# Two changes to a three-stage kernel: the first 256 tokens run through the network with float32 products, and the first solve stays on VectorE

## The chip, the cores and the metric

One NeuronCore of a Trainium2 chip runs the whole program; the other cores idle. The metric is the device time of one execution in microseconds (us). Engines are written as in the profile: PE is TensorE, PEld its loads of stationary operands, DVE is VectorE, ACT is ScalarE, POOL is GpSimd, SP is the queue that issues nearly all transfers.

## The reference, cut to what matters

Three stages follow each other; the first is a recurrence over 768 positions for 32 heads, the other two are networks over the 3072 tokens that it leaves.

```python
for t in range(S):                                   # 4 batches, 8 heads, S=768, D=48
    y[:, :, t] = einsum('bhd,bhde->bhe', q[:, :, t], state)
    v_old = einsum('bhde,bhd->bhe', state, k_n[:, :, t])
    state = state + beta_t * outer(k_n[:, :, t], v[:, :, t] - v_old)
x = y as (3072, 384)
g = s * relu(x @ w_in)**2 + b                        # w_in 384 x 2048, float64 in memory
x = g @ w_out                                        # w_out 2048 x 384, float64 in memory
e = argmax over 8 experts of the cosine of x and expert_emb
out = gate * relu(x @ w1[e]) @ w2[e]                 # 384 x 1024 x 384
```

## The kernel before, in words

**Stage one, the recurrence.** Positions are cut into chunks of C=32. Four chunks of all heads form a group `gi`; there are six, of 512 tokens each. For a group the kernel transposes keys and queries (`tr_kn` or `tr_k`, `tr_q`), forms their products (`gram`, for the first group `gram_first`), moves them into one 32x32 problem per lane of VectorE (`lanes_in`) and inverts a unit triangular matrix there. `solve(gi, j)` is one of 31 steps over the whole 32x32 matrix: a product into `tmp` and a subtraction from `T`, both on VectorE. For groups 0 and 1 the kernel takes another way: `solve_d` does 15 such steps on the two 16x16 diagonal blocks at once, and the block below them is made by TensorE: `off_in` transposes twice, `off_1` and `off_2` are 32 products per chunk each, with an eviction between them. The result is `tt`. Then four `dstep`s per group go through the chunks, each a chain: `ks` (TensorE, state times keys), X (VectorE), `tx` (TensorE, with `tt`), bdu (VectorE), `ku` (TensorE), the state `sst` (VectorE); `mu` makes the output tokens, which ACT copies to `x_t`.

**Stage two, the first network,** is `moe1`, over twelve groups `kk` of 256 tokens. `x_split` transposes the tokens and splits them into a high and a low part in fp32r (`xh`, `xl`). `mm1(kk, j)`, j from 0 to 7, does 256 of the 2048 hidden features: 6 pairs (f, m), and for each three fp32r matmuls (high by high, high weight by low x, low weight by high x). ACT takes relu, POOL squares and applies s and b, ACT and VectorE split the result into `gh` and `gl`. `mm2(kk, j)` is 18 fp32r matmuls into `acc`. Both are generators with six steps of three matmuls; a group has 96 steps. `mm2(kk, j)` is emitted after `mm1` of two pairs later.

**Weights.** They come as float64, in 16 pieces of 128 x 768 values (even pieces of `w_in`, odd of `w_out`; `W_ORDER` is the order of use). A piece is turned into float32 by two ACT scalings (`w_scale`), two VectorE bit operations and one POOL addition into a separate buffer `wa`; then `w_parts` has ACT cast the high part and POOL subtract for the low part. `convert` does this in two `w_step`s per piece, `convert_piece` both. `poll` lets group 1 of the tokens be split only when all pieces are converted.

**Order.** On PE, DVE, ACT and POOL the order of emission is the order of execution. `attention` holds a list of items with due times for each group, and yields between them; the main loop then calls `run_moe(n)`, which emits n steps of `moe1`, and every fifth step one `w_step`. While group 0 is in its four chunks there are no tokens yet; the items there are the rest of `off_2`, `k_rows` and eight conversions. Items with times from 99 on prepare group 1: transposes, `gram`, the router, `lanes_in(1)`, 15 `solve_d`, `off_in`, `off_1` and `off_2`; after each the main loop emits 2, 12, 3, 10 or 1 steps of `moe1`, 97 in all, which is the whole of token group 0 and the start of group 1. From `gi=1` on the number of steps for each quarter of a hop is set by what is left (24*KF//2*gi - 36 steps by the end of a group). `warm` are matmuls without a use for their result. Transfers are issued by SP in an order that the framework chooses near the order of emission.

Of the kernel before, what the change touches and what calls it, by code (L numbers as in the profile page):

```python
# [19 lines left out]
def tile_kernel(ctx, tc, q, k, v, beta, w_in, w_out, s_in, b_in, emb, tau, w1, w2, out):  # L20
# [60 lines left out]
    def xh_ring(shape, dt, name):  # L81
        t = mp.tile([128, 2, KD, TT], dt, tag="xhl", name=name, bufs=2)
        if len(shape) == 4:
            return t
        return t.rearrange("p a k t -> p (a k t)")[:, 0:shape[1] * shape[2]].rearrange("p (a b) -> p a b", b=shape[2])
# [111 lines left out]
    def gc_tile(gi):  # L197
        if gi == 1:
            gc_t[gi] = att.tile([128, B, 2, HG, C], F32, tag="kqt", name="gc", bufs=KQB)
        elif gi:  # L200
            gc_t[gi] = stg.tile([128, B, 2, HG, C], F32, tag="gc", name="gc")
        else:
            gc_t[gi] = xh_ring([128, 32, C], F32, "gc").rearrange("p (h g n) t -> p h g n t", h=B, g=2)
# [40 lines left out]
    def lanes_in(gi):  # L244
        if gi < 2:
            Af = stg.tile([128, C + 1, C], F32, tag="A", name="A")
            Tf = T0[0] if gi == 0 else stg.tile([128, C + 1, C], F32, tag="gc", name="T")
# [4 lines left out]
        if gi > 1:  # L252
            Tf = T = stg.tile([128, C, C], F32, tag="gc", name="T")
# [63 lines left out]
    def off_in(gi):  # L317
        A, T = ln.pop(gi)
        tt_t[gi] = att.tile([128, 2 * HG * B, C], F32, tag="tt", name="tt", bufs=2)
# [5 lines left out]
    def off_1(gi, n0, n1):  # L325
# [8 lines left out]
        if gi:  # L334
            zz = stg.tile([128, 2 * B, n1 - n0, C2], F32, tag="tmp", name="zz")
        else:
            if n0 == 0:
                of["z"] = mp.tile([128, 2, TT], F32, tag="gl", name="zz", bufs=2).rearrange(
                    "p a t -> p (a t)").rearrange("p (n e i) -> p n e i", n=HG, i=C2)
            zz = of["z"][:, n0].unsqueeze(2)  # L340
# [133 lines left out]
    def attention(more, first):  # L474
        for gi in range(NG):
# [5 lines left out]
            if gi == 0:  # L481
                add(0, off_2, 0, 1, 2)
                add(0, first)
                add(0.1, k_rows, 0, 1)
                add(1, off_2, 0, 2, 3)
                add(1.1, convert_piece)
                add(2, off_2, 0, 3, 4)
                add(2.1, k_rows, 0, 2)
                add(4.1, k_rows, 0, 3)
                for i in range(3, 3 * HG - 2):  # L490
                    if i % 3 != 2:
                        add(i, convert_piece)
                add(10, convert_piece)
            if gi + 1 < NG:
# [747 lines left out]
```

## Time and profile before

| | before |
|---|---|
| three timed runs | 1018.87, 1020.95, 1022.46 us; median 1020.95 us |
| the profiled execution | 1018.81 us, of it 1017.1 us between first and last instruction |
| mean granted clock of TensorE | 0.917 of full |
| busy, share of the span | PE 86%, PEld 79%, DVE 48%, ACT 32%, POOL 30% |
| chain that ended last | the last three instructions on the output, 0.1% each |

The chain of waits reaches back only to the last output tile, so it does not say what bounds the middle; the windows and the waits of TensorE do. A busy share of PE counts pipelined matmuls as one block; mean ns of one matmul includes the latency that overlaps its neighbours, and the price of one in a row is busy time over count.

### The profile page before, as it was taken

To read this page: it belongs to the slowest core of one execution; us is meant where nothing else is said; L and a number is where in the kernel's file an instruction comes from. 1 tells how busy PE (TensorE), PEld (TensorE's weight loads), DVE (VectorE), ACT (ScalarE), POOL (GpSimd) and SP (SyncE) were. 2 spreads that over 40 slices of the span, in tenths; PEclk is the share of its full clock that TensorE was granted. 3 is DMA by queue.
4 is the path that set the end of the run, shared out by engine and by line. 5 is a ranking of instruction groups with operands and counts; after the bars stand their busy time and mean duration, and the time that the engine had idled before them with its cause. 6 is when DMAs were issued, how large, how long until landed. Compare 5 with 4: busy or idle time off the path is not lost. (4 is left out here: it accounts for less than half of the span.)

```text
span 1017.1 us, 29943 instructions
## 1 busy us (share of the span) xinstructions
PE 875.7 (86%) x13213; PEld 801.1 (79%) x13213; DVE 484.9 (48%) x984; ACT 324.7 (32%) x689; POOL 301.8 (30%) x294
## 2 busy tenths in 40 slices
PE   6468646496699799979998999999998889889997
PEld 4355646495599799979898889999997679779896
DVE  3638499425953596259725873224414333331111
ACT  2127634123135133423342333334422222222221
POOL 4116568312122333233323333334540110110100
PEclk7558788679699899999999999999999999999999
DMA  8791133001122012101200000003202901114000
GB/s 149 219 291 30 25 50 60 3 19 34 23 45 49 3 36 46 41 11 34 48 18 3 18 2 17 3 17 94 79 17 49 42 24 51 51 36 175 16 32 24
DMA packets 119826, 50.35 MB, mean 50 GB/s; under 512 B 94167, under 2 KB 116368, under 8 KB 119696
## 3 DMA queue, kind: packets, MB, share of 16 engines
q1 hardware_dynamic: 112784, 47.23, 20.2%
q10 hardware_dynamic: 6336, 1.18, 0.8%
q8 instruction: 104, 1.70, 0.7%
q14 instruction: 26, 0.21, 0.1%
q0 software_dynamic: 576, 0.02, 0.0%
HBM read 38.84 MB, written 9.74 MB: 48 GB/s over the span
## 5 line engine op out<-in xcount | busy, mean ns | idle before, releaser
L678 PE MATMUL h<-xhl,wp 128*128 128x256 f32 x1728 | 250.9, 295 | 43.4 <-ACT r L686 29.8
L678 PEld LDWEIGHTS h<-xhl,wp 128*128 128x128 f32 x1728 | 224.0, 199 | 50.4 <-ACT r L686 32.6
L687 POOL TENSOR_TENSOR r<-r 128x512 f32<-128x512 f32 x96 | 106.3, 1108 | 350.8 <-ACT r L686 350.8
L710 PE MATMUL acc<-gh,wp 128*128 128x256 f32 x1152 | 161.4, 286 | 1.7 <-POOL wp L595 1.7
L710 PEld LDWEIGHTS acc<-gh,wp 128*128 128x128 f32 x1152 | 146.1, 193 | 3.4 <-POOL wp L595 2.0
L690 DVE TENSOR_TENSOR gl<-r,gh 128x512 fp32r<-128x512 f32 x96 | 74.2, 773 | 130.6 <-ACT gh L689 130.4
L689 ACT CAST gh<-r 128x512 fp32r<-128x512 f32 x96 | 59.8, 623 | 161.0 <-POOL r L688 158.3
L952 DVE SCALAR_TENSOR_TENSOR hl<-h,hh 128x512 fp32r<-128x512 f32 x46 | 31.7, 691 | 139.2 <-ACT hh L951 139.2
L686 ACT ACTIVATE r<-h 128x512 f32<-128x512 f32 x96 | 57.4, 598 | 97.3 <-PE h L678 69.5
L710 PE MATMUL acc<-gl,wp 128*128 128x256 f32 x576 | 84.6, 283 | 0.2 <-DVE gl L690 0.2
L688 POOL TENSOR_SCALAR r<-r,s_sb,b_sb 128x512 f32<-128x512 f32 x96 | 81.1, 845 | 10.0
L710 PEld LDWEIGHTS acc<-gl,wp 128*128 128x128 f32 x576 | 75.2, 193 | 0.5 <-DVE gl L690 0.4
L437 ACT COPY x<-ch 32x384 f32<-32x384 f32 x96 | 45.2, 471 | 69.7 <-PE ch L423 68.7
L1021 POOL TENSOR_TENSOR x2l<-xr,x2h 128x512 fp32r<-128x512 f32 x15 | 18.7, 1279 | 164.0 <-ACT x2h L1020 164.0
L1032 PE MATMUL o<-w2h,hh 128*128 128x384 f32 x184 | 62.3, 339 | 0.0
L1032 PE MATMUL o<-w2l,hh 128*128 128x384 f32 x184 | 61.9, 336 | 0.0
L1032 PE MATMUL o<-w2h,hl 128*128 128x384 f32 x184 | 61.8, 336 | 0.0
L292 DVE TENSOR_TENSOR T<-T,tmp 128x31 f32<-128x31 f32 (+15 forms) x124 | 54.6, 440 | 4.3
L289 DVE TENSOR_TENSOR tmp<-A,T 128x31 f32<-128x31 f32 (+15 forms) x124 | 55.1, 445 | 2.9
L949 PE MATMUL h<-x2l,w1h 128*128 128x512 f32 x120 | 49.6, 414 | 6.5 <-POOL x2l L1021 6.5
L951 ACT ACTIVATE hh<-h 128x512 fp32r<-128x512 f32 x46 | 27.4, 598 | 83.4 <-PE h L949 83.4
L949 PE MATMUL h<-x2h,w1h 128*128 128x512 f32 x120 | 48.4, 403 | 6.1 <-ACT x2h L1020 4.9
(212 smaller groups left out, 1260.3 us busy)
## 6 DMA issues: line engine op xcount, KB each, us to landing
wr<-in_moe_w_in SPq DMA_DIRECT2D x16, 384.0 KB
wr<-in_moe_w_out SPq DMA_DIRECT2D x8, 768.0 KB
v<-in_v SPq DMA_DIRECT2D x192, 24.0 KB
x2d<-x2s SPq DMA_DIRECT2D x24, 192.0 KB
out<-o SPq DMA_DIRECT2D x24, 192.0 KB
qpad<-in_q SPq DMA_DIRECT2D x40, 96.0 KB
kpad<-in_k SPq DMA_DIRECT2D x160, 24.0 KB
xr<-x2d SPq DMA_DIRECT2D x5, 768.0 KB
```

Of the source, the lines that this page charges most:

```text
L289: nc.vector.tensor_tensor(out=tmp, in0=A[:, j + 1:, j:j + 1].to_broadcast([128, m, j + 1]), in1=T[:, j:j + 1, 0:j + 1].to_broadcast([128, ...
L292: nc.vector.tensor_tensor(out=T[:, j + 1:, 0:j + 1], in0=T[:, j + 1:, 0:j + 1], in1=tmp, op=ALU.subtract)
L437: nc.scalar.copy(out=x_t[gi][pb:pb + C, :, r * 96:(r + 1) * 96].rearrange("p h (g e) -> p h g e", g=2), in_=y[32 * rr:32 * rr + 32, :, :, ...
L678: nc.tensor.matmul(out=h[:, f, :], lhsT=wi_(w, 2 * j + f, m), rhs=x[:, m, :], start=(m == 0 and i == 0), stop=(m == KD - 1 and i == 2))
L686: nc.scalar.activation(out=r, in_=h, func=AF.Relu)
L687: nc.gpsimd.tensor_tensor(out=t, in0=r, in1=r, op=ALU.mult)
L688: nc.gpsimd.tensor_scalar(out=t, in0=t, scalar1=s_sb, scalar2=b_sb, op0=ALU.mult, op1=ALU.add)
L689: later.append((step[0] + 7, lambda: nc.scalar.copy(out=gh, in_=t)))
L690: later.append((step[0] + 9, lambda: nc.vector.tensor_tensor(out=gl, in0=t, in1=gh.bitcast(F32), op=ALU.subtract)))
L710: nc.tensor.matmul(out=acc[:, m * TT:(m + 1) * TT], lhsT=wo_(w, 2 * j + f, m * 128, 128), rhs=x[:, f, :], start=(j == 0 and m not in seen ...
L949: nc.tensor.matmul(out=ps, lhsT=w[:, m, f * 128:(f + 1) * 128], rhs=x[:, m, :], start=(m == 0 and i == 0), stop=(m == KD - 1 and i == 2))
L1032: nc.tensor.matmul(out=ps, lhsT=h[:, sl], rhs=w[:, f, :], start=(f == 0 and i == 0), stop=(f == KF2 - 1 and i == 2))
```

## The change

It has two parts that share memory and order. The first group of the recurrence is inverted by 31 `solve` steps and one transpose (`lanes_out`); `solve_d`, `off_in`, `off_1` and `off_2` stay for group 1 only. The keys of group 1 are loaded once, in the layout of `load_k`, ahead of queries, beta and values, and all `k_rows` of group 0 come before the solve. Token group 0 goes through the network with float32 matmuls on whole weights: 6 in `mm1` and 6 in `mm2` for each j, with a step each, and relu, square and the affine map on ACT. A weight piece is converted in place (`x_step`), where float32 values lie in every second word, and the matmuls of group 0 read them there (`wx_`). `split_step` makes the two fp32r parts later, ACT for the high and VectorE for the low part, into the place of the piece before it in `W_ORDER`, once group 0 has used that one. Every fifth step of `moe1` calls one `x_step`, or, when all pieces are converted, one `split_step`. Cut to its core:

```diff
             if gi == 0:
-                add(0, off_2, 0, 1, 2)
                 add(0, first)
-                add(0.1, k_rows, 0, 1)
-                add(1, off_2, 0, 2, 3)
-                add(1.1, convert_piece)
-                add(2, off_2, 0, 3, 4)
-                add(2.1, k_rows, 0, 2)
-                add(4.1, k_rows, 0, 3)
-                for i in range(3, 3 * HG - 2):
+                for i in range(1, 3 * HG - 1):
                     if i % 3 != 2:
-                        add(i, convert_piece)
-                add(10, convert_piece)
+                        add(i, x_step)
...
-                    for i in range(B):
-                        add(99 if i < 2 else 100, tr_kn, 1, i)
-                    add(100, load_k, 1, [nc.sync])
-                    for f in (tr_q, gram):
+                    add(99, second_places)
+                    for f in (tr_k, tr_q, gram):
                         for s in range(0, HG, 2 if f is gram else 1):
-                            add(100, f, 1, s)
+                            add(99 if f is tr_k and s < 2 else 100, f, 1, s)
...
+    def x_step():
+        n = cv["n"]
...
+        cv["n"] += 1
+        w_scale(n + 3)
+        lo, hi = w_words(n)
+        nc.vector.scalar_tensor_tensor(out=lo, in0=hi, scalar=-2147483648, in1=lo,
+                                       op0=ALU.bitwise_and, op1=ALU.bitwise_or)
+        nc.vector.tensor_scalar(out=hi, in0=hi, scalar1=3, scalar2=None, op0=ALU.logical_shift_left)
+        nc.gpsimd.tensor_tensor(out=hi, in0=hi, in1=lo, op=ALU.add)
+
+    def split_step():
+        n = cv["s"]
+        if n >= NU or (n and used[n - 1] < 2) or cv["n"] < NU:
+            return
+        cv["s"] += 1
+        w = wpool.tile([128, 2, 2, DM], F32R, tag=f"w{W_ORDER[n - 1]}" if n else "ws", name=f"wp{W_ORDER[n]}")
+        x = w_raw[W_ORDER[n]].rearrange("p c (f two) -> p c f two", two=2)[:, :, :, 1].bitcast(F32)
         nc.scalar.copy(out=w[:, :, 0], in_=x)
-        nc.gpsimd.tensor_tensor(out=w[:, :, 1], in0=x, in1=w[:, :, 0].bitcast(F32), op=ALU.subtract)
...
+    def w_next():
+        if cv["n"] < NU:
+            x_step()
+        else:
+            split_step()
 
     def w_need(j):
         while j not in wpp:
-            w_step()
+            split_step()
         return wpp[j]
 
+    def wx_(j, ff, c):
+        while j not in W_ORDER[:cv["n"]]:
+            x_step()
+        return w_raw[j][:, ff % 2].rearrange("p (f two) -> p f two", two=2)[:, c:c + 128, 1].bitcast(F32)
+
...
+    def second_places():
+        tt_t[1] = att.tile([128, 2 * HG * B, C], F32, tag="tt", name="tt", bufs=2)
+        pl["xl"] = att.tile([128, 2 * HG * B * C], F32R, tag="tt", name="xl1", bufs=2)[:, 0:KD * TT].rearrange(
+            "p (m t) -> p m t", m=KD)
...
-            x = xh_ring([128, 2, KD, TT], F32R, "xhl")
-            xT_t[t] = (x[:, 0], x[:, 1])
+            if t == 0:
+                xT_t[0] = (x_half(0, F32, "x0"), None)
+            elif t == 1:
+                xT_t[1] = (x_half(1, F32R, "xh"), pl["xl"])
+            elif t % 2:
+                xT_t[t] = (x_half(0, F32R, "xh"), x_half(1, F32R, "xl"))
+            else:
+                x = wpool.tile([128, 2, KD, TT], F32R, tag=f"w{W_ORDER[-1]}", name="xhl")
+                xT_t[t] = (x[:, 0], x[:, 1])
...
-        nc.vector.tensor_tensor(out=xl[:, :, sl], in0=pp, in1=xh[:, :, sl].bitcast(F32), op=ALU.subtract)
+        if t:
+            nc.vector.tensor_tensor(out=xl[:, :, sl], in0=pp, in1=xh[:, :, sl].bitcast(F32), op=ALU.subtract)
...
-        if p < 2 * NHG and p // 2 <= st["pos"] + 1 and (p < 2 or cv["n"] > NU):
+        if p < 2 * NHG and p // 2 <= st["pos"] + 1 and (p < 4 or cv["s"] == NU):
...
-                    for i, (w, x) in enumerate(((0, xh), (0, xl), (1, xh))):
+                    if kk == 0:
+                        nc.tensor.matmul(out=h[:, f, :], lhsT=wx_(2 * j, 2 * j + f, m * 128), rhs=xh[:, m, :],
+                                         start=(m == 0), stop=(m == KD - 1))
+                    for i, (w, x) in enumerate(((0, xh), (0, xl), (1, xh)) if kk else ()):
                         nc.tensor.matmul(out=h[:, f, :], lhsT=wi_(w, 2 * j + f, m), rhs=x[:, m, :],
                                          start=(m == 0 and i == 0), stop=(m == KD - 1 and i == 2))
...
+                if kk == 0:
+                    used[W_ORDER.index(2 * j)] += 1
             t = r = mp.tile([128, 2, TT], F32, tag="r", name="r", bufs=2)
+            if kk == 0:
+                gf = mp.tile([128, 2, TT], F32, tag="gh", name="gf", bufs=2)
+                nc.scalar.activation(out=r, in_=h, func=AF.Relu)
+                nc.scalar.activation(out=r, in_=r, func=AF.Square)
+                later.append((step[0] + 6, lambda: nc.scalar.activation(
+                    out=gf, in_=r, func=AF.Identity, scale=s_sb, bias=b_sb)))
+                g_t[kk, j] = (gf, None)
+                yield
+                tick()
+                return
             gh = mp.tile([128, 2, TT], F32R, tag="gh", name="gh", bufs=2)
...
+            if kk:
+                seq = [(f, m, w, gh) for f in range(2) for m in range(KD) for w in range(2)]
+                seq += [(f, m, 0, gl) for f in range(2) for m in range(KD)]
+            else:
+                seq = [(f, m, 0, gh) for f in range(2) for m in range(KD)]
...
-                nc.tensor.matmul(out=acc[:, m * TT:(m + 1) * TT], lhsT=wo_(w, 2 * j + f, m * 128, 128), rhs=x[:, f, :],
+                nc.tensor.matmul(out=acc[:, m * TT:(m + 1) * TT], lhsT=wo_(w, 2 * j + f, m * 128, 128) if kk else wx_(
+                    2 * j + 1, 2 * j + f, m * 128), rhs=x[:, f, :],
...
-                if i % 3 == 2:
+                if i % 3 == 2 or kk == 0:
                     yield
                     tick()
+            if kk == 0:
+                used[W_ORDER.index(2 * j + 1)] = 2
...
-                while pos and cv["n"] <= NU:
-                    w_step()
+                while pos > 1 and cv["s"] < NU:
+                    split_step()
...
-        load_n(1, kpad[1], k, nc.sync)
         for i in W_ORDER[8:]:
             w_load(i)
+        router_setup_a()
+        load_k(1, sy)
...
-        router_setup_a()
-        k_rows(0, 0)
-        w_scale(2)
+        for s in range(HG):
+            k_rows(0, s)
+        w_scale(7)
...
-        for j in range(C2 - 1):
-            solve_d(0, j)
-            if j == 7:
+        for j in range(C - 1):
+            solve(0, j)
+            if j == 26:
...
                                  start=True, stop=True)
-                warm(12)
-        off_in(0)
-        for n in range(3):
-            off_1(0, n, n + 1)
-        convert_piece()
-        off_2(0, 0, 1)
-        off_1(0, 3, 4)
+                warm(9)
+        lanes_out(0)
+        x_step()
...
                 if state["n"] % 5 == 0:
-                    w_step()
+                    w_next()
```

Left out are the places of the tiles: `gc` of group 0 moves from the ring of `xh`/`xl` to the ring of `kqt`, `T` and `A` of group 0 lose their 33rd row, `zz` of group 0 and `wa` go, `tt` of group 1 is allocated in `second_places`.

## Rows read from the trace of the kernel before

**Rows 1.** Page, part 2: busy tenths of TensorE in 40 slices.

```profile
PE   6468646496699799979998999999998889889997
```

**Rows 2.** Windows: length, busy us of PE, PEld, DVE, ACT, POOL; clock, DMA share.

```profile
51.80:75.80 24.00, 14.32 (x491) 12.52 (x483) 8.26 (x15) 4.95 (x9) 4.08 (x2) 0.50 0.95 300
...
109.80:144.00 34.20, 27.84 (x422) 26.04 (x423) 21.51 (x42) 17.45 (x42) 16.18 (x13) 0.87 0.22 38
144.00:190.00 46.00, 17.51 (x118) 16.38 (x116) 41.87 (x49) 15.52 (x23) 35.15 (x24) 0.78 0.25 43
190.00:207.50 17.50, 15.99 (x555) 13.66 (x555) 2.82 (x6) 2.18 (x6) 2.67 (x3) 0.70 0.02 5
207.50:283.40 75.90, 58.98 (x1380) 53.52 (x1379) 47.49 (x110) 20.97 (x55) 13.30 (x13) 0.80 0.14 27
...
400.00:1017.10 617.10, 577.52 (x6666) 536.75 (x6664) 240.65 (x516) 189.28 (x390) 151.32 (x152) 0.98 0.16 38
```

**Rows 3.** Waits of TensorE, 88 to 208 us: us in total, times, longest.

```profile
PE h L678 <- ACT r L686: 14.7, 5, 8.5
PE h L678 <- ACT xhl L643: 13.3, 2, 12.8
...
PE ep L805 <- DVE x2s L798: 4.6, 1, 4.6
```

**Rows 4.** Timeline of VectorE, the solves of groups 0 and 2: start, us.

```profile
26.54 0.19 DVE L309 TENSOR_TENSOR tmp<-A,T 128x30 f32<-128x30 f32 x1
...
32.81 1.48 DVE L312 TENSOR_TENSOR T<-T,tmp 128x110 f32<-128x110 f32 x1
...
37.56 1.92 DVE L320 STREAM_TRANSPOSE tt<-T 128x1024 f32<-128x1024 f32 x1
...
268.33 0.42 DVE L289 TENSOR_TENSOR tmp<-A,T 128x256 f32<-128x256 f32 x1
268.78 0.42 DVE L292 TENSOR_TENSOR T<-T,tmp 128x256 f32<-128x256 f32 x1
...
283.27 0.19 DVE L289 TENSOR_TENSOR tmp<-A,T 128x31 f32<-128x31 f32 x1
```

**Rows 5.** Timeline of TensorE, 51 to 208 us.

```profile
51.78 1.29 PE L388 MATMUL u<-v,tt 32*32 32x48 f32 x51
...
75.81 1.50 PE L388 MATMUL u<-X,tt 32*32 32x48 f32 x64
...
84.85 1.00 PE L388 MATMUL u<-X,tt 32*32 32x48 f32 x64 [0.82 <-DVE X L373]
...
98.37 0.88 PE L423 MATMUL ch<-bdu,mt 32*32 32x48 f32 x64
...
109.81 2.03 PE L678 MATMUL h<-xhl,wp 128*128 128x256 f32 x6 [0.57 <-ACT xhl L643]
...
207.45 1.96 PE L367 MATMUL ch<-sst,kqt 48*64 48x48 f32 x64
```

**Rows 6.** Waits of TensorE with no releaser shown, 38 to 76 us.

```profile
PE z L351 <- issue: 9.1, 3, 3.3
PE z L332 <- issue: 4.6, 1, 4.6
```

**Rows 7.** Timeline of SP: issues of keys in the layout of load_k.

```profile
121.07 32.62 SPq L120 DMA_DIRECT2D kpad<-in_k  x64
```

**Rows 8.** Groups of TensorE by shape: count | busy us, mean ns | idle.

```profile
L678 PE MATMUL h<-xhl,wp 128*128 128x256 f32 x1728 | 250.9, 295 | 43.4 <-ACT r L686 29.8 <-ACT xhl L643 13.3
...
L1065 PE MATMUL hr<-xp,w1p 128*128 128x128 f32 x48 | 5.8, 277 | 0.0
...
L1072 PE MATMUL or<-w2p__11383,hp 128*128 128x384 f32 x16 | 5.3, 486 | 0.0
```

**Rows 9.** Groups of VectorE and ACT.

```profile
L690 DVE TENSOR_TENSOR gl<-r,gh 128x512 fp32r<-128x512 f32 x96 | 74.2, 773 | 130.6 <-ACT gh L689 130.4
...
L594 ACT CAST wp<-wa 128x768 fp32r<-128x768 f32 x16 | 13.3, 830 | 24.1 <-POOL wa L610 24.1
```

More of the change, by code (lines that the diff above doesn't have):

```diff
@@ L79, in wo_, with x_half @@
         return w_need(ff // 2 * 2 + 1)[:, ff % 2, part, c:c + n]
[L81 to L85, printed above, removed]
+    def x_half(i, dt, name):
+        return mp.tile([128, KD, TT], dt, tag=f"x{i}", name=name)
     kpad = [att.tile([128, B, HG, DP], F32, name=f"kpad{i}") for i in range(2)]
@@ L244, in lanes_in @@
     def lanes_in(gi):
-        if gi < 2:
+        if gi == 1:
             Af = stg.tile([128, C + 1, C], F32, tag="A", name="A")
-            Tf = T0[0] if gi == 0 else stg.tile([128, C + 1, C], F32, tag="gc", name="T")
+            Tf = stg.tile([128, C + 1, C], F32, tag="gc", name="T")
             A, T = Af[:, 0:C], Tf[:, 0:C]
@@ L251, in lanes_in @@
         nc.vector.transpose(out=A, in_=gc_t[gi].rearrange("p h g n t -> p t (h g n)"))
-        if gi > 1:
-            Tf = T = stg.tile([128, C, C], F32, tag="gc", name="T")
+        if gi != 1:
+            Tf = T = stg.tile([128, C, C], F32, tag="gc", name="T") if gi else T0[0]
         if gi:
@@ L574, in w_load @@
             nc.sync.dma_start(out=raw.rearrange("p c (f two) -> p c f two", two=2), in_=wo64[:, ff:ff + 2, :, :])
-    cv = {"n": 0, "a": 0}
+    cv = {"n": 0, "a": 0, "s": 0}
     NU = NPC // 2
@@ L588, in w_scale @@
             nc.scalar.activation(out=lo, in_=lo.bitcast(mybir.dt.uint32), func=AF.Copy, scale=2.0 ** -29)
-    def w_parts(n):
-        j = W_ORDER[n]
-        w = wpool.tile([128, 2, 2, DM], F32R, tag=f"w{j}", name=f"wp{j}")
-        x = wa[:, n % 2].rearrange("p (c f) -> p c f", c=2).bitcast(F32)
-        nc.scalar.copy(out=w[:, :, 0], in_=x)
-        nc.gpsimd.tensor_tensor(out=w[:, :, 1], in0=x, in1=w[:, :, 0].bitcast(F32), op=ALU.subtract)
-        wpp[j] = w
-    def convert():
-        for n in range(NU + 1):
-            w_scale(n + 2)
-            if n < NU:
-                lo, hi = w_words(n)
-                nc.vector.scalar_tensor_tensor(out=lo, in0=hi, scalar=-2147483648, in1=lo,
-                                               op0=ALU.bitwise_and, op1=ALU.bitwise_or)
-                yield
-            if n:
-                w_parts(n - 1)
-            if n < NU:
-                nc.vector.tensor_scalar(out=hi, in0=hi, scalar1=3, scalar2=None, op0=ALU.logical_shift_left)
-                nc.gpsimd.tensor_tensor(out=wa[:, n % 2], in0=hi, in1=lo, op=ALU.add)
-                yield
-        cv["n"] = NU + 1
@@ L614, in tile_kernel @@
-    cg_ = convert()
-    def w_step():
-        next(cg_, None)
-    def convert_piece():
-        w_step()
-        w_step()
+    used = [0] * NU
+    def x_step():
+        n = cv["n"]
+        if n >= NU:
+            return
[6 more added lines that the diff above has]
+        nc.gpsimd.tensor_tensor(out=hi, in0=hi, in1=lo, op=ALU.add)
@@ L703, in mm2 @@
             last = j == KF // 2 - 1
-            seq = [(f, m, w, gh) for f in range(2) for m in range(KD) for w in range(2)]
-            seq += [(f, m, 0, gl) for f in range(2) for m in range(KD)]
+            if kk:
+                seq = [(f, m, w, gh) for f in range(2) for m in range(KD) for w in range(2)]
+                seq += [(f, m, 0, gl) for f in range(2) for m in range(KD)]
+            else:
+                seq = [(f, m, 0, gh) for f in range(2) for m in range(KD)]
             left = {m: sum(x[1] == m for x in seq) for m in range(KD)}
```

25 lines of the change are left out of this document (8 added, 17 removed).

## The prediction

> **What bounds the kernel now.** I read the tenths of the page first, for where TensorE has holes; then windows around the changed stages, for which engine is full there; then TensorE's waits between 88 and 208 us; then the timelines of VectorE and TensorE, for the chains.
>
> The reader should see three things. TensorE is at 90% or more in most slices from the twelfth on, and at four to eight tenths in ten of the eleven before [rows 1]. From 400 us to the end it is busy 577.5 of 617.1 us at a clock of 0.98, its upper level, 2.4 GHz [rows 2]: there the kernel costs what its matmuls cost, and this change takes none of them away. So time can only be won in the first 283 us, and what is won there arrives at the end as a shift. The worst hole is 144 to 190 us: TensorE 17.5 of 46 us, VectorE 41.9, POOL 35.2 [rows 2]. The conversion of weights, squares, splits and the second solve share two elementwise engines there, and TensorE waits 14.7 us for the relu that frees `h` and 13.3 us for the first tokens of group 1, of which one wait is 12.8 us [rows 3]: `poll` holds them until the last piece is converted. A smaller hole lies before 76 us: the clock is 0.50 (its lower level, 1.2 GHz), the DMA share 0.95 [rows 2].
>
> **The first solve.** Removed are 15 steps, from 26.54 to 37.56 us [rows 4], the two transposes and the block products; `tx` of chunk 0 starts at 51.78 us [rows 5]. Added are 31 steps, 62 instructions. In group 2 one over 31 elements takes 0.19 us, one over 256 takes 0.42 us and 0.45 from start to start [rows 4], so a gap of 0.03 goes on each. The mean product has 176 elements (sum of (31-j)(j+1) over 31); between the two rows that is 0.22 + 0.23 x 145/225 = 0.37 us, and 62 of them 22.9 us. Two operations ran about 1.2 us long in the old solve, of which one is shown (1.48 us for 110 elements [rows 4]), while POOL scaled the values; that happens again: 25.3 us. From 26.54 this ends at 51.8, and one transpose of 1.92 us [rows 4] leads to `tx` at 53.8 us. The first `x_step` behind it on VectorE runs under `tx`. So the longer solve costs 2 us, and no more, because the old way then waited for 256 small products. Below nothing it can hardly be: the operations are counted.
>
> **The four chunks.** From the first `tx` to the second went 24.0 us (51.78 to 75.81), from there to the next 9.0 us (84.85) [rows 5]. In the first, `off_2` and two `k_rows` stood in TensorE's order, and stretches in which it waited for nothing the profile names: 9.1 us in `off_2` and 4.6 in `off_1` over 38 to 76 us [rows 6]. All of these go or move ahead of the solve. A chunk without them costs 9.0; the weights still come in at a share of 0.95 with the clock at 0.50 [rows 2], so I take 11, with 9 and 24 as bounds. The rest, 75.81 to 99.25 (98.37 plus 0.88) [rows 5], is 23.4 us and stays: the `x_step`s do the same two VectorE operations as before, with one POOL operation in place of two. End of the chunks: 53.8 + 11 + 23.4 = 88.2, against 99.25.
>
> **Keys of group 1.** `load_k` is 32 transfers, put on SP behind the weights and ahead of queries, beta and values of group 1. Of the same kind 64 took 32.6 us to issue [rows 7], so 16.3 us. The old load of these keys (8 transfers) goes from in front of the last weights, and the late `load_k` from behind. Behind the new one wait queries, needed by `tr_q` after about 95 us, and values, needed only after `lanes_in(1)`. I cost it at nothing, since the first reader, `tr_k`, comes at 88 us; without this cover each microsecond late counts in full. ACT gets a new wait: `w_scale(7)` needs seven pieces there at once. Behind it stands no work until the copies of the first `mu`, near 60 us, and the chain of VectorE needs ACT nowhere in between: nothing.
>
> **Token group 0 in float32.** A float32 matmul shows as two records: the 24 calls at L1065 are 48 records of 5.8/48 = 0.121 us for 128 columns, the 8 at L1072 are 16 of 0.331 us for 384 [rows 8]. For 256 columns that is between 2 x 0.331 x 256/384 = 0.44 and 2 x 2 x 0.121 = 0.48 us. Three fp32r matmuls cost 3 x 250.9/1728 = 0.44 us in the mean, cold stretches included [rows 8]. So 84 steps of token group 0, those emitted before group 1's first, cost 38 us instead of 37: TensorE's work stays, its waits go. Those rows read stationary operands without gaps; `wx_` reads every second word, which no row shows. The lower bound is 0.44; for the upper one each of the two stationary loads takes 2 x 0.121 us (the whole record at L1065, twice) and hides under nothing: 0.45 + 0.48 = 0.93 us. I take 0.45, since the two known shapes ran with their loads under the matmuls before them.
>
> FP8 and Floating Point Precision of the Trainium skill (TensorE Precision Notes) has float32 as four passes of the array; an estimate from it at 2.4 GHz is 4 x 256/2.4 = 0.43 us, 36 us for 84, two less than by the rows. It speaks against the change all the same: four passes replace three. SBUF — State Buffer of the skill (Door 1) says that two accesses to a 16-byte line suffice for full bandwidth; every second float32 word is just that, so by it the stationary loads would cost nothing more, which no row here can show.
>
> **From the chunks to group 1's first `ks`.** Before, `mm1` began at 109.81, 10.6 us after the last `mu`; `ks` of group 1 followed at 207.45 [rows 5]. The 10.6 us hold copies queued behind conversions on ACT; I take 8.5: 96.7. In the 97.7 us up to `ks` TensorE was busy 27.8 + 17.5 + 16.0 = 61.3 us [rows 2]. With 38 for 37 that is 62.3. Of its idle time the waits for relu between the first three `mm1` stay (2 us), the wait for the router (4.6 [rows 3]), and some 2 us among `off_1` and `off_2`: 71 us, `ks` at 167.7.
>
> The other engines just fit under that. VectorE was busy 21.5 + 41.9 = 63.4 us between 109.8 and 190 us [rows 2], with the same eight conversions, `lanes_in`, solve, transposes and router. It loses eight `gl` of 0.773 us (6.2) and gets about eleven of the 16 splits (95 steps make 19 calls, eight of them conversions) at 0.773 x 1.5 = 1.16 us, 12.8 [rows 9]: 70 us. That is an upper bound, since many of its operations ran long beside POOL, and POOL loses `w_parts` and both operations of token group 0; below, I take 55. ACT gets two operations per j and keeps its casts of 0.83 us [rows 9]; it was busy 33 of 80 us [rows 2].
>
> **Sum.** `ks` of group 1 moves from 207.45 to 167.7, 39.8 us. Five splits and two steps of `moe1` fall into the 75.9 us of group 1's chunks, where VectorE is in the chain (47.5 us busy [rows 2]): 3 us back. Net 37 us. The profiled execution took 1018.8 us, 0.2% below the median of 1020.95; 1020.95 - 37 = 984 us.
>
> **The rivals.** (1) More: a first chunk of 9.0, `mm1` 6 us after `mu`, and TensorE at 2.4 GHz through the stretch, where it was granted 0.70 to 0.87 [rows 2]: the 61.3 us shrink by a fifth, 12. With 2 + 2.5 more that is 967 us. For it: the clock was low where TensorE had holes. Against: the wait-laden small products stay. (2) The strided stationary operand costs the upper bound: 84 x 0.48 = 40 us back, 1024 us: in sum about nothing. Against: records of 0.22 us leave room to load under them. (3) Slower: a split puts a cast on ACT behind relu, which waits for TensorE, and a subtraction on VectorE behind the cast, with `solve_d` behind that; before, the subtraction stood on POOL. If each of eleven holds VectorE for d us, its stretch is 63.4 - 6.2 + 11d = 57 + 11d. Against 71 us and the 37 won this decides from d = 4.6 us; at one whole `mm1` with its wait, 6 us, the stretch is 123 and the time 984 + 52 = 1036 us. Against: 45 steps of `moe1` are emitted beside the solve anyway, so a VectorE in step with TensorE ends soon after it. (4) Less: the shift is partly eaten; five splits in group 1's chunks hold the chain 2 us more each, and the keys of group 1 come 8 us late: 37 - 18 = 19, 1002 us. For it: those transfers are small and stand behind the weights; against: 20 us of slack by the sum above.
>
> **How the numbers follow.** Forecast 984 (its own range 974 to 995) 0.53; more 0.14; less 0.17; no gain by strides 0.06; slower by splits 0.10. Faster and slower count from 0.3%, about 3 us, what this kernel's three runs can tell from no change. Faster: 0.53 + 0.14 + 0.17 = 0.84. The stride case lies on both sides of no change: 0.05 of it counts as same and 0.01 as slower, with the splits 0.11. For 8 in 10 the range takes in both "more" and "less" and stops short of the stride case: 962 to 1010.
>
> **What would show it.** Right: `tx` of chunk 0 near 54 us, the last `mu` near 88, `mm1` from 97, float32 records of 0.22 us, no wait of 12.8 us for tokens of group 1, `ks` of group 1 near 168, and stretches after 400 us as long as now. Wrong: float32 records well over 0.25 us in a row, VectorE idle behind casts among `solve_d`, `tr_k` waiting for a transfer, or a gain at `ks` that is gone at 283 us less the shift.

## The result, and the profile after

The changed kernel takes 990.58 us (median of four runs, 989.89 to 992.01) against 1019.91 (1018.33 to 1022.46): ratio 0.971, 95% interval 0.969 to 0.974, a gain of 29.3 us where 37 were forecast. The profiled execution has a span of 989.1 us at a mean granted clock of 0.924.

TensorE's timeline of the changed kernel gives the milestones of [rows 5] (start, duration, call; in brackets the idle time before and its releaser):

```profile
54.69 1.16 PE L376 MATMUL u<-v,tt 32*32 32x48 f32 x64 [1.12 <-DVE tt L293]
...
64.43 1.33 PE L376 MATMUL u<-X,tt 32*32 32x48 f32 x53 [0.73 <-DVE X L361]
...
85.31 0.88 PE L411 MATMUL ch<-bdu,mt 32*32 32x48 f32 x64
...
92.78 1.19 PE L674 MATMUL h<-x,wr 128*128 128x256 f32 x2 [0.66 <-ACT x L638]
...
174.51 1.96 PE L355 MATMUL ch<-sst,kqt 48*64 48x48 f32 x64
```

| | before | predicted | after |
|---|---|---|---|
| first `tx` | 51.78 | 53.8 | 54.69 |
| end of the last `mu` of group 0 | 99.25 | 88.2 | 86.19 |
| first `mm1` | 109.81 | 96.7 | 92.78 |
| first `ks` of group 1 | 207.45 | 167.7 | 174.51 |
| first `ks` of group 2 | 283.42 | 246.6 | 253.4 |
| end of the span | 1017.1 | 980 | 989.1 |

The windows of the changed kernel stand against [rows 2] (length, busy us of PE, PEld, DVE, ACT, POOL; clock, DMA share, GB/s):

```profile
92.80:117.40 24.60, 17.58 (x321) 14.28 (x322) 10.62 (x23) 15.53 (x39) 5.34 (x3) 0.91 0.21 34
117.40:156.50 39.10, 32.49 (x133) 28.33 (x132) 35.69 (x64) 21.57 (x30) 12.77 (x8) 0.87 0.31 55
156.50:174.50 18.00, 16.49 (x542) 12.12 (x540) 6.68 (x9) 4.80 (x9) 2.39 (x2) 0.66 0.12 21
...
371.00:989.10 618.10, 582.59 (x6658) 541.46 (x6656) 240.58 (x516) 188.96 (x390) 151.01 (x151) 0.97 0.16 37
```

The 97.7 us from `mm1` to `ks` are 81.7 now, not 71. From 371 us on nothing changed: as many operations of VectorE (516) as before from 400 us on, in 618 us against 617, with TensorE 94% busy in both. TensorE's waits in the stretch, against [rows 3] (us in total, times, longest):

```profile
PE h L674 <- ACT r L687: 8.8, 3, 6.6
PE ep L822 <- DVE x2s L815: 3.9, 1, 3.9
```

The wait of 12.8 us for the first tokens of group 1 is gone, and the waits for relu fell from 14.7 to 8.8 us. One wait of 6.6 us, from 137.5 to 144.1, looks like the culprit for the missing 10 us. ACT's timeline tells where it comes from:

```profile
142.59 0.88 ACT L589 CAST wp<-wr 128x768 fp32r<-128x768 f32 x1 [9.37 <-DVE wp L590]
143.37 0.59 ACT L687 ACTIVATE r<-h 128x512 f32<-128x512 f32 x1
```

The cast of the second split writes where the first piece lay, so it waits for that piece's subtraction on VectorE; relu stands behind the cast, and TensorE behind relu. VectorE's timeline shows what the subtraction (L590, 141.55) stood behind:

```profile
119.16 1.98 DVE L246 STREAM_TRANSPOSE A<-gc 128x1024 f32<-128x1024 f32 x1
...
132.59 0.19 DVE L304 TENSOR_TENSOR tmp<-A,T 128x30 f32<-128x30 f32 x1
132.81 1.47 DVE L307 TENSOR_TENSOR T<-T,tmp 128x30 f32<-128x30 f32 x1
134.18 0.95 DVE L577 SCALAR_TENSOR_TENSOR wr<-wr 128x768 int32<-128x768 int32 x1
135.16 0.56 DVE L579 TENSOR_SCALAR wr<-wr 128x768 int32<-128x768 int32 x1
...
141.36 0.28 DVE L307 TENSOR_TENSOR T<-T,tmp 128x110 f32<-128x110 f32 x1
141.55 0.95 DVE L590 TENSOR_TENSOR wp<-wr,wp 128x768 fp32r<-128x768 f32 x1
...
154.40 2.01 DVE L314 STREAM_TRANSPOSE tt<-T 128x1024 f32<-128x1024 f32 x1
156.26 2.07 DVE L316 STREAM_TRANSPOSE dd<-T 128x1024 f32<-128x1024 f32 x1
```

Two readings are open. Either the wait of 6.6 us is the loss, or VectorE's queue from `lanes_in` (119) to the transposes (154.4) is, and the wait only a sign of it. TensorE's timeline shows how the two hang together:

```profile
144.10 5.02 PE L674 MATMUL h<-x,wr 128*128 128x256 f32 x12 [6.61 <-ACT r L687]
...
157.88 0.73 PE L326 MATMUL z<-tt,gc 32*32 32x16 f32 x64
```

After the wait TensorE works without a pause up to the first product of `off_1` at 157.88, only 1.5 us after the transpose into `tt` has ended (154.40 plus 2.01). So the queue holds up `ks` in two ways of nearly equal length, through the wait and through `tt`; by this timeline at most 1.5 us could be won if the wait alone went. Most of the experiments change the queue; none takes away the wait alone.

### The profile page after: what moved, and what is told of

The parts are those of the page before. It is cut to its first block, busy times and chain, and to the rows that moved or that the text cites. A ratio compares the mean times of both kernels' runs of the same rounds, so it can differ in the third digit from the quotient of the medians.

```text
span 989.1 us, 28725 instructions
## 1 busy us (share of the span) xinstructions
PE 879.0 (89%) x12602; PEld 799.1 (81%) x12602; DVE 477.5 (48%) x1009; ACT 331.9 (34%) x689; POOL 251.8 (25%) x262
## 5 line engine op out<-in xcount | busy, mean ns | idle before, releaser
L698 POOL TENSOR_TENSOR r<-r 128x512 f32<-128x512 f32 x88 | 96.1, 1092 | 356.9 <-ACT r L697 356.9
L724 PE MATMUL acc<-gh,wp 128*128 128x256 f32 x1056 | 146.2, 284 | 0.0
L677 PE MATMUL h<-xh,wp 128*128 128x256 f32 x576 | 124.5, 298 | 11.7 <-ACT r L697 11.7
L724 PEld LDWEIGHTS acc<-gh,wp 128*128 128x128 f32 x1056 | 133.7, 193 | 1.2
L701 DVE TENSOR_TENSOR gl<-r,gh 128x512 fp32r<-128x512 f32 x88 | 63.0, 716 | 128.6 <-ACT gh L700 128.5
L677 PEld LDWEIGHTS h<-xh,wp 128*128 128x128 f32 x576 | 98.3, 198 | 14.3 <-ACT r L697 12.7
L677 PE MATMUL h<-xhl,wp 128*128 128x256 f32 x720 | 101.5, 288 | 3.3 <-ACT r L697 3.3
L965 DVE SCALAR_TENSOR_TENSOR hl<-h,hh 128x512 fp32r<-128x512 f32 x46 | 31.7, 691 | 141.5 <-ACT hh L964 141.5
L677 PEld LDWEIGHTS h<-xhl,wp 128*128 128x128 f32 x720 | 90.0, 190 | 5.3 <-ACT r L697 3.9
L677 PE MATMUL h<-xl,wp 128*128 128x256 f32 x288 | 83.0, 288 | 0.0
L699 POOL TENSOR_SCALAR r<-r,s_sb,b_sb 128x512 f32<-128x512 f32 x88 | 74.9, 851 | 9.2
L287 DVE TENSOR_TENSOR T<-T,tmp 128x31 f32<-128x31 f32 (+15 forms) x155 | 69.4, 448 | 5.3
L1045 PE MATMUL o<-w2h,hh 128*128 128x384 f32 x184 | 62.3, 339 | 0.0
L1034 POOL TENSOR_TENSOR x2l<-xr,x2h 128x512 fp32r<-128x512 f32 x15 | 18.7, 1279 | 166.3 <-ACT x2h L1033 166.3
```

Source lines behind the costliest of these rows:

```text
L287: nc.vector.tensor_tensor(out=T[:, j + 1:, 0:j + 1], in0=T[:, j + 1:, 0:j + 1], in1=tmp, op=ALU.subtract)
L677: nc.tensor.matmul(out=h[:, f, :], lhsT=wi_(w, 2 * j + f, m), rhs=x[:, m, :], start=(m == 0 and i == 0), stop=(m == KD - 1 and i == 2))
L698: nc.gpsimd.tensor_tensor(out=t, in0=r, in1=r, op=ALU.mult)
L699: nc.gpsimd.tensor_scalar(out=t, in0=t, scalar1=s_sb, scalar2=b_sb, op0=ALU.mult, op1=ALU.add)
L701: later.append((step[0] + 9, lambda: nc.vector.tensor_tensor(out=gl, in0=t, in1=gh.bitcast(F32), op=ALU.subtract)))
L724: nc.tensor.matmul(out=acc[:, m * TT:(m + 1) * TT], lhsT=wo_(w, 2 * j + f, m * 128, 128) if kk else wx_(2 * j + 1, 2 * j + f, m * 128), rh ...
```

## The experiments

Their runs are compared with runs of the kernel before on the same chip, whose median was 1020.2 us for the first four, 1020.7 for the next four, 1021.6 for the three after and 1022.2 for the last. "`tt`" is the start of the transpose into `tt` of group 1 on VectorE (L314 in the changed kernel), "`ks`" the first of group 1. At the end of the section a table has all of them. Each kernel was profiled once (the early router twice, as two runs). The starts differ: kernels whose program is the changed one up to the first `mm1` reached it between 89.1 and 92.9 us, the changed kernel itself at 92.78, and no run shows why. So `tt` and `ks` are also read from `mm1` on; in the changed kernel these are 61.6 and 81.7 us. In the two runs of the early router the second came out at 79.5 and 78.7.

**One part alone: the long first solve.** Made from the kernel before; `solve_d`, `off_in`, `off_1` and `off_2` of group 0 go, all else stays.

```diff
-        for j in range(C2 - 1):
-            solve_d(0, j)
+        for j in range(C - 1):
+            solve(0, j)
...
-        off_in(0)
-        for n in range(3):
-            off_1(0, n, n + 1)
+        lanes_out(0)
```

> The kernel before with one part of the change alone: group 0 is inverted by 31 whole steps and one transpose, the block products of group 0 go; weights, token group 0 and the keys of group 1 stay as before. Theory (two shifts that add): the chunks of group 0 end near 89 us instead of 99, the conversions move with them, and the whole is 9 to 12 us faster, about 1009 us. Rival (the conversion of 16 pieces alone sets when group 1 starts, and the first solve changes nothing behind it): ks of group 1 stays within 3 us of 207 and the time within 4 us of 1020.

It took 1015.89 us, ratio 0.9955 (0.9934 to 0.9976), less than half of what was expected. The first `tx` came at 54.45, the last `mu` ended at 94.28 (99.25 before) and `ks` stood at 202.44, 5.0 us earlier, of which 4.5 reached the end. So the shift arrives in full, but the solve itself makes only 5.0 of the 13.1 us that the whole change wins by the last `mu`. From `mm1` to `ks` it is 98.6 us here, against 97.6 before. For the rest the other part is needed. What in it does that was not tested; two candidates are `k_rows` before the solve, and conversions with one POOL operation, beside which VectorE's shift takes 0.56 us each where most of these took 1.7 to 2.07.

**The other part alone: float32 for token group 0.** The changed kernel with the old first solve.

> The changed kernel with the old first solve (15 steps on the diagonal blocks, block products, the old places of k_rows), all else as changed. Theory (two shifts that add): chunks end near 98 us as before the change, the stretch from there to ks of group 1 takes 88 us as after it, and the time is about 1002 us. Rival (the gain is all in token group 0, and the longer solve only buys memory): within 4 us of 991.

998.63 us, ratio 0.9765 (0.9721 to 0.9809). The last `mu` ended at 94.58, not near 98, and `ks` stood at 183.6. So this part alone wins 21.6 us at the end and 23.9 at `ks`, the solve alone 4.3 and 5.0, and both together 29.3 and 32.9. That leaves 3 to 4 us that only both bring; the four runs here spread from 994.8 to 1003.0, so this rest is not settled.

**The subtraction of the splits on POOL.**

```diff
-        nc.vector.tensor_tensor(out=w[:, :, 1], in0=x, ...
+        nc.gpsimd.tensor_tensor(out=w[:, :, 1], in0=x, ...
```

> The changed kernel with the subtraction of split_step on POOL instead of VectorE. Theory (the wait of 6.6 us of TensorE at 137 us comes from a cast on ACT that waits for the subtraction of the piece before, which stands behind conversions and solve steps on VectorE): the wait falls under 2 us and the time by 3 to 7 us, to about 986 us. Rival (POOL beside the solve stretches solve steps from 0.3 to 1.4 us as it did before the change): eleven splits cost VectorE as much as they give, time within 2 us of 991 or above.

992.27 us, ratio 0.9728 (0.969 to 0.9766), the longest wait still 6.27 us. POOL's timeline shows why:

```profile
136.70 1.46 POOL L580 TENSOR_TENSOR wr<-wr 128x768 int32<-128x768 int32 x1 [2.17 <-DVE wr L579]
138.12 1.86 POOL L590 TENSOR_TENSOR wp<-wr,wp 128x768 fp32r<-128x768 f32 x1
```

The subtraction now stands behind the addition of the last conversion, which waits for VectorE's shift; and the solve's steps beside POOL take 1.8 to 1.9 us each. VectorE, busy 53.3 us from `mm1` to `ks` against 53.0, lost no work by the edit. `tt` came at 154.36, as without the edit, but `mm1` had begun 3.6 us sooner: from there to `tt` it is 65.2 us, against 61.6.

**The late conversions earlier**, at every third step of `moe1`.

```diff
-                if state["n"] % 5 == 0:
+                if state["n"] % (3 if cv["n"] < NU else 5) == 0:
```

> The changed kernel with the eight late conversions at every third step of moe1 instead of every fifth, so that six of them fall where VectorE is idle at 88 to 112 us, and the splits begin at step 25 instead of 45. Theory (VectorE was about 9 us behind ACT when the second split asked for it): the wait of 6.6 us shrinks to 3 or less and the time falls by 3 to 6 us, to about 987 us. Rival (the scalings on ACT come in front of the copies and relu that TensorE waits for at 92 to 110 us): those waits grow by as much, time within 2 us of 991.

991.01 us, ratio 0.970 (0.967 to 0.9731). The wait fell from 6.6 to 4.5 us, and nothing was won: `tt` at 154.71, `ks` at 175.2, and from `mm1` to `ks` 83.7 us against 81.7. Splits took the conversions' place on VectorE: nine subtractions stand ahead of `tt` where there were seven. A shorter wait with a longer queue won nothing, which speaks for the queue.

**Work taken off VectorE's queue.** Three edits: splits that begin only in group 1's chunks unless a product needs one; the same with the early conversions; and the router's small operations, 3.2 us of VectorE from 113.8 to 117.0, moved to where it idles. A fourth kernel has all three.

```diff
-        else:
+        elif st["gi"]:
             split_step()
...
+                    add(99, router_setup_a2)
                     add(99, second_places)
...
-                    add(102, router_setup_a2)
```

> Left as it is but for the splits of the weights, which begin only in the first chunk of group 1 unless a product needs one sooner. Theory: VectorE's queue, not one wait of TensorE, sets the end of group 1's preparation; the seven subtractions of 0.95 us that stand ahead of the first transpose of tt (154.4 us after the change) go, so that it starts at about 148 and the first state product of group 1 at about 168 to 170 instead of 174.5. What they then cost in the chunks of group 1 decides the time: if the chunks have room, about 985 us; if they give all of it back, 991. Rival: TensorE's 66.6 us of work and its cold stretches set the stretch; the first transpose of tt comes earlier, but the first state product stays at about 174 and the time within 2 us of 990.6.

> The late splits, and the last conversions at every third step instead of every fifth. Theory (VectorE's queue): as the late splits alone or up to 2 us better at the first state product (166 to 170), since the conversions take the same time on VectorE, only sooner. Rival (the wait of TensorE for relu behind the cast): that wait is gone in both, and the first state product comes at the same time as with the late splits alone.

> After the change, with the router's small VectorE operations (4.3 us from 112.4 to about 118) put ahead of group 1's key transposes, where VectorE idles (88.5 to 95). Theory (VectorE's queue): first transpose of tt about 3 to 4 us earlier, at 150 to 151, first state product at 170.5 to 171.5, and about 987 us; TensorE's wait for ep (3.94 us) goes. Rival: TensorE takes the time as another wait or as a lower clock, the first state product stays within 1 us of 174.5 and the time within 1.5 us of 990.6; or the operations wait there for the transfer of the router's rows and push the key splits back.

> All three edits together. Theory: the gains on VectorE's queue add, 6 + 3.5 us of it ahead of the transposes of tt: first state product at 164 to 167, and 980 to 986 us depending on what group 1's chunks give back. Rival: TensorE's own work of 66.6 us becomes the bound, and the first state product does not come before 168; the time stays at or above 986.

`tt` moved to 148.2, 139.3, 151.3 and 140.2, `ks` to 171.0, 166.3, 171.1 and 162.2. From `mm1` to `tt`, 6.3 us were won for seven subtractions taken off (6.7 us), 13.8 with the early conversions too, 2.0 for the router's 3.2 us: the queue decides about `tt`, and does so with the early router although TensorE's wait for relu grew there to 9.6 us. For `ks` it decides only up to a point. From `mm1` to `ks` 3.6, 6.9, 2.3 and 12.0 us were won, with late splits much less than at `tt`. The timelines with late splits and early conversions show why, first VectorE's, then TensorE's:

```profile
141.16 2.02 DVE L316 STREAM_TRANSPOSE dd<-T 128x1024 f32<-128x1024 f32 x1
148.75 0.96 DVE L590 TENSOR_TENSOR wp<-wr,wp 128x768 fp32r<-128x768 f32 x1 [5.57 <-ACT wp L589]
```

```profile
115.10 0.45 PE L822 MATMUL ep<-ident,x2s 8*128 8x8 f32 x3 [3.02 <-DVE x2s L815]
115.48 5.49 PE L724 MATMUL acc<-gf,wr 128*128 128x256 f32 x12
...
144.29 2.75 PE L724 MATMUL acc<-gf,wr 128*128 128x256 f32 x12
148.77 0.39 PE L677 MATMUL h<-xh,wp 128*128 128x256 f32 x1 [1.73 <-ACT wp L589]
...
150.79 0.73 PE L326 MATMUL z<-tt,gc 32*32 32x16 f32 x64
```

The transposes end at 143.18. TensorE, without a pause since 115.10, has matmuls of token group 0 ahead of `off_1` until 147.04, waits for a split that now begins only when a product needs it, and starts `off_1` 7.6 us after the transposes. There TensorE's own order is the bound. The router's edit on top of these two confirms it: from `mm1` to `tt` it changes nothing (47.8 us in both), but to `ks` it wins 5.1 us, as TensorE's wait of 3.0 us for the router goes, and with it a restart at a granted clock of 0.50, in which twelve records took 5.49 us instead of 2.75. With all three edits TensorE is busy 65.0 of 69.8 us.

The late splits are also paid again. The first `ks` of group 2 follows that of group 1 by 83.9, 82.4 and 82.9 us in the three kernels that have them, against 78.9 in the changed kernel and 80.4 and 78.0 with the early router alone. In the first chunk of group 1 TensorE then waits for a split, and works on at the lower clock: over the 10 us from `ks` on it was granted 0.50, in the changed kernel 0.76. From one matmul to the next it takes 0.21 us there, later 0.12. Its timeline with late splits alone:

```profile
175.66 0.58 PE L677 MATMUL h<-xh,wp 128*128 128x256 f32 x1 [1.54 <-ACT wp L589]
...
177.25 0.41 PE L677 MATMUL h<-xl,wp 128*128 128x256 f32 x1
177.46 0.63 PE L677 MATMUL h<-xh,wp 128*128 128x256 f32 x2
```

So late splits alone won 3.5 us at `ks`, gave 5 back, and took 994.09 us (0.9718, 0.9692 to 0.9744); with early conversions 991.8 (0.9727, 0.9708 to 0.9745). All three edits took 982.89 us, ratio 0.9617 (0.959 to 0.9643), below the interval of the changed kernel; in the profiled execution, with a clock of 0.921 against 0.924, 12.3 us at `ks`, 8.3 at group 2 and 7.3 at the end are left. These milestones weigh more than the interval, as the last run below shows.

**Work put on it.** Eight operations of 0.57 us whose result nobody reads, between two steps of group 1's solve: in the changed kernel, and in that with all three edits.

```diff
+                    add(312.5, vec_more)
...
+    def vec_more():
+        vm = x2s[0][0:NE, :, 1, NE:]
+        for _ in range(8):
+            nc.vector.tensor_tensor(out=vm, in0=vm, in1=vm, op=ALU.subtract)
```

> The changed kernel with eight small VectorE operations more (about 0.53 us each by the router's row of the same shape, 4.3 us in all; nobody waits for their result) put between two steps of group 1's solve. Theory (VectorE's queue sets the end of group 1's preparation): the first transpose of tt goes from 154.4 to about 158.5 and the first state product from 174.5 to 177.5 to 179; the time to 993 to 995 us. Rival (TensorE sets it): the first state product stays within 1 us of 174.5 and the time within 1.5 us of 990.6.

> The same eight operations in the kernel with all three edits, whose first state product came at 162.2. Theory: VectorE still sets the transposes there (24.7 us busy of the 26.6 from 117.4 to 144), so the first transpose of tt goes from 140.2 to about 144.4 and the first state product to about 166; 985 to 987 us. Rival: by then TensorE has become the bound, and neither moves by over 1 us.

In the changed kernel 4.6 us more on VectorE moved `tt` by 4.4 and `ks` by 4.8, to 179.3 (from `mm1` on by 5.4 and 5.9), and the time to 998.27 (0.9775, 0.9754 to 0.9795). At `ks` of group 2 4.4 us are left; at the end 7.5 in the profiled executions, 7.7 in the medians. That is more than was put in, and where the rest comes from is open; the chip may have a part in it, as in the last run below. VectorE's timeline of it:

```profile
151.03 4.60 DVE L809 TENSOR_TENSOR x2s<-x2s 8x384 f32<-8x384 f32 x8
...
158.76 1.94 DVE L314 STREAM_TRANSPOSE tt<-T 128x1024 f32<-128x1024 f32 x1
```

With all three edits `tt` moved only by 1.3 and `ks` by 2.2 against the kernel without the load, which seems to be the rival. VectorE's timelines of the two say otherwise. First without the load, then with it:

```profile
130.24 0.19 DVE L304 TENSOR_TENSOR tmp<-A,T 128x30 f32<-128x30 f32 x1
...
140.17 1.99 DVE L314 STREAM_TRANSPOSE tt<-T 128x1024 f32<-128x1024 f32 x1
141.99 2.01 DVE L316 STREAM_TRANSPOSE dd<-T 128x1024 f32<-128x1024 f32 x1
...
149.19 0.35 DVE L343 SCALAR_TENSOR_TENSOR tt<-z,negm,tt 128x128 f32<-128x128 f32 x1 [2.68 <-PE z L339]
...
161.15 0.35 DVE L343 SCALAR_TENSOR_TENSOR tt<-z,negm,tt 128x128 f32<-128x128 f32 x1 [3.92 <-PE z L339]
```

```profile
127.14 0.19 DVE L304 TENSOR_TENSOR tmp<-A,T 128x30 f32<-128x30 f32 x1
...
135.99 4.60 DVE L809 TENSOR_TENSOR x2s<-x2s 8x384 f32<-8x384 f32 x8
...
141.46 1.96 DVE L314 STREAM_TRANSPOSE tt<-T 128x1024 f32<-128x1024 f32 x1
```

From the first step to `tt` it is 9.93 us without and 14.32 with the load: 4.4 of the 4.6 arrive. That profiled execution simply reached the solve 3.1 us sooner; its last `mu` already ended 2.8 us earlier, ahead of the edit. From `mm1` to `ks` it is 75.2 us with the load, 69.8 without. Without it the transposes end at 144.0 and TensorE's float32 matmuls ahead of `off_1` at 143.8: the two are level there, and more work on the queue still reaches `ks`. The times named in advance were missed all the same. Its time, 989.9 (0.9697, 0.9677 to 0.9718), is 7.0 us longer, on another chip.

**Early router and early conversions**, with the splits where the change has them.

> The router's small operations early and the last conversions at every third step, with the splits of the weights where the change has them. Theory (VectorE's queue; conversions only change places with splits, and late splits are paid again in group 1's chunks): as the early router alone, first state product at 170 to 172 and 982 to 986 us. Rival (the 9.6 us for which TensorE waited for relu with the early router alone are a loss of their own): those go, and the first state product comes at 165 to 168, about 980 us.

`tt` at 149.0, `ks` at 168.8, 5.7 us earlier than in the changed kernel and between the two expectations. But 3.6 of the 5.7 lie ahead of `mm1`; from there to `ks` it is 79.6 us, as with the early router alone, so the conversions won nothing, as the theory had it. Its rival was not tested, since TensorE still waited 7.9 us in one piece for relu. The time was no better: 992.61 us, ratio 0.9722 (0.9701 to 0.9744). The profiled execution, 989.1 us, had a clock of 0.929; the timed ones between 992 and 995 had 0.917 to 0.922.

**The early router again.** With that edit alone four of the timed runs took 982 to 984 us and one 986.6, but the profiled one 990.99.

> The kernel with the early router a second time, on another chip. Its median was 983.2 us with a granted clock of 0.928 to 0.933 in the quick executions, while its profiled execution took 991.0 at 0.922 and stood only 0.2 us ahead of the changed kernel at its end. Reading one (the 7 us are the edit's): median again 981 to 985. Reading two (the 3.4 us at the first state product of group 1 are mostly given back, and the rest was a higher granted clock on that chip): median 987 to 991, at 0.92 to 0.925.

989.89 us (985.08 to 991.41), ratio 0.9675 (0.9651 to 0.9699): reading two. Together the twelve runs of this kernel go from 982.03 at a mean clock of 0.933 to 991.4 at 0.927 and 991.2 at 0.922. The two intervals, 0.9617 to 0.9644 and 0.9651 to 0.9699, do not even overlap. A gain under some 7 us is not settled by such runs, however narrow the interval of one chip; the milestones in the rows settle it better. This kernel has `ks` at 171.1 and 170.4, 3.4 to 4.1 us early, and 0.2 to 1.2 left at the end.

| kernel | `mm1` | `tt` | `ks` | `mm1` to `ks` | `ks` of group 2 | span | median |
|---|---|---|---|---|---|---|---|
| before | 109.8 | 182.5 | 207.5 | 97.6 | 283.4 | 1017.1 | 1019.91 |
| long first solve alone | 103.8 | 176.7 | 202.4 | 98.6 | 278.3 | 1012.6 | 1015.89 |
| float32 alone | 101.1 | 163.3 | 183.6 | 82.4 | 262.0 | 1001.3 | 998.63 |
| changed | 92.8 | 154.4 | 174.5 | 81.7 | 253.4 | 989.1 | 990.58 |
| subtraction on POOL | 89.1 | 154.4 | 175.7 | 86.6 | 254.8 | 990.5 | 992.27 |
| early conversions | 91.5 | 154.7 | 175.2 | 83.7 | 254.9 | 991.0 | 991.01 |
| late splits | 92.9 | 148.2 | 171.0 | 78.1 | 254.9 | 995.3 | 994.09 |
| late splits, early conversions | 91.5 | 139.3 | 166.3 | 74.9 | 248.8 | 988.9 | 991.8 |
| early router | 91.6 | 151.3 | 171.1 | 79.5 | 251.5 | 988.9 | 983.24 |
| early router again | 91.7 | 150.8 | 170.4 | 78.7 | 248.5 | 987.9 | 989.89 |
| early router, early conversions | 89.2 | 149.0 | 168.8 | 79.6 | 249.0 | 987.2 | 992.61 |
| all three | 92.4 | 140.2 | 162.2 | 69.8 | 245.1 | 981.8 | 982.89 |
| changed, more on VectorE | 91.7 | 158.8 | 179.3 | 87.6 | 257.8 | 996.6 | 998.27 |
| all three, more on VectorE | 89.2 | 141.5 | 164.4 | 75.2 | 248.2 | 987.3 | 989.9 |

## Why the prediction was right, and where a size was off

The measured 990.58 us lies in the forecast's own range of 974 to 995; the gain was 29.3 us where 37 were forecast.

**The first solve: right.** VectorE's timeline of the changed kernel:

```profile
26.79 0.19 DVE L284 TENSOR_TENSOR tmp<-A,T 128x31 f32<-128x31 f32 x1
...
32.31 1.53 DVE L287 TENSOR_TENSOR T<-T,tmp 128x207 f32<-128x207 f32 x1
33.88 1.54 DVE L284 TENSOR_TENSOR tmp<-A,T 128x220 f32<-128x220 f32 x1
...
52.50 1.93 DVE L293 STREAM_TRANSPOSE tt<-T 128x1024 f32<-128x1024 f32 x1
```

62 operations took 25.7 us (25.3 forecast), with two stretched ones as before, and `tx` came 0.9 us after the forecast.

**The chunks: 2 us better.** From the first `tx` to the second went 9.7 us, not 11; the rest took 21.8, not 23.4. Why is not shown: the conversions ran shorter (their shifts took 0.56 us), but between kernels with the same program up to there the chunks went from 28.2 to 31.7 us, here 31.5, against 34.4 forecast.

**Keys: right.** TensorE waited about 0.5 us for transfers at `tr_k`.

**float32 with strided operands: right,** and the rival of 1024 us is dead. The row of the group (count | busy us, mean ns | idle):

```profile
L674 PE MATMUL h<-x,wr 128*128 128x256 f32 x96 | 26.9, 426 | 9.5 <-ACT r L687 8.8 <-ACT x L638 0.7
```

and in TensorE's timeline a stretch in which it never paused:

```profile
121.79 2.75 PE L674 MATMUL h<-x,wr 128*128 128x256 f32 x12
124.38 2.75 PE L724 MATMUL acc<-gf,wr 128*128 128x256 f32 x12
```

Twelve records, six matmuls, take 2.59 us from start to start: 0.432 us for a matmul against 0.45 forecast, with the stationary operand at every second word. The page FP8 and Floating Point Precision of the Trainium skill (TensorE Precision Notes) has four passes for float32; the estimate from it, 4 x 256 columns at 2.4 GHz, is 0.43 us, and the trace agrees.

**From `mm1` to `ks`: the mis-sized term.** Forecast 71 us, measured 81.7. Of the 10.7 us, 4.3 are work of TensorE: it was busy 66.6 us, against 62.3. What these consist of was not separated; restarts have a part in them, as the twelve records behind the waits of 3.9 and 6.6 us took 4.55 and 5.02 us at granted clocks of 0.61 and 0.54, where they take 2.75 at full clock. The other 6.5 are idle time: 15.1 us against 8.6. The waits for relu alone were 8.8 us against 2; the prediction kept 2 of the 14.7 us of before, as the other engines were to fit under TensorE's work. The step that failed stands in the prediction as "The other engines just fit under that": VectorE's busy time was summed over the whole stretch and compared with TensorE's. It was busy only 53.0 of 81.7 us, less than the lower estimate, and bound it all the same, because the stretch is three pieces behind each other. Up to 117 us VectorE has little to do (10.6 of 24.6 us), as `lanes_in` needs the products of `gram`. From there to the transposes it is full, 35.7 of 39.1 us. Behind them, 18 us of `off_1`, eviction and `off_2` follow in turn. The splits themselves were as forecast: eleven before `ks`, 0.96 us each against 1.16. Work put on the middle piece (4.6 us) moved `tt`, counted from `mm1`, by 5.4 and 4.4, and seven splits taken off it (6.7 us) by 6.3. With all three edits the stretch takes 69.8 us, about the 71 of the forecast; by then TensorE's own work is nearly all of it.

**The slower rival: its mechanism was there, its price was not.** A cast on ACT did stand ahead of relu and behind VectorE, for one wait of 6.6 us, but each split held VectorE for about 1 us, far from the 4.6 from which that rival decides.

**Behind `ks`: about right.** Group 1's chunks gave 2.9 us back against 3 forecast. 2.0 more went between group 2 and the end of this profiled execution; between two executions of one kernel such sizes occur (2.4 us in the same chunks with the early router), so no cause is claimed, and the agreement of 2.9 with 3 may be chance. In all the forecast of 984 missed by 6.6 us. By the time of `ks` 10.7 were lost in the term above and 3.9 won ahead of it; that the second hid part of the first is luck.

## What to carry to other kernels

Compare engines stage by stage, between the points where one hands over to the next: an engine with idle time over the stretch can still be the bound of the piece in its middle. A long wait of the busiest engine may only show where another queue is full; take work off that queue, or put some on, and see whether the end of the stage follows. Count from the start of the stage, not from the start of the kernel: `mm1` began up to 3.7 us apart in kernels that differ only behind it. A queue that is relieved soon hands the bound to the next engine, here to TensorE. Work that is moved out of a full stage is won only if its new place has room: the splits moved into the next chunks cost there 3.6 to 5.0 us against the changed kernel.

## What the runs showed of the hardware

An operation of VectorE with two operands from SBUF, started beside one of POOL that reads SBUF too, ended with it. POOL's timeline of the changed kernel:

```profile
132.75 1.47 POOL L580 TENSOR_TENSOR wr<-wr 128x768 int32<-128x768 int32 x1 [0.50 <-DVE wr L579]
135.80 1.47 POOL L580 TENSOR_TENSOR wr<-wr 128x768 int32<-128x768 int32 x1 [1.59 <-DVE wr L579]
```

VectorE's subtraction of 30 elements, started at 132.81, takes 1.47 us and ends at 134.28, POOL's at 134.22; without POOL beside it such a step takes 0.19 to 0.22. SBUF — State Buffer of the Trainium skill (Who interferes with whom) says that the second of the two is blocked until the first is done; the trace agrees.

In the 18 us with the 32x32 products of `off_1` and `off_2` the granted clock was 0.66 of full, although TensorE was busy 16.5 us of them.

Executions of one kernel on one chip differ by up to 9 us with the mean granted clock (982.03 at 0.933, 990.99 at 0.922); on another chip the same kernel took 985.08 and 987.93 us at 0.930.
